# Batch 0 of a windowed attention: transposes a pair ahead, one pair without bias tables, v cast on GpSimd

## The chip, the core and the metric

The kernel runs on one core of a Trainium2 chip. The metric is the device time of one execution in microseconds. The engines are named as in the profile: PE (TensorE matmuls), PEld (its weight loads), DVE (VectorE), ACT (ScalarE), POOL (GpSimd) and SP (SyncE, which here only issues DMAs). Each engine works through its own list of instructions in order and waits on semaphores of the others.

## The reference

Attention over 8 batches, 8 heads, 576 positions of 64 elements, with a linear distance bias and a causal window of 128; then a two-layer MLP over the 4608 tokens:

```python
scores = scale * np.matmul(q, k.transpose(0, 1, 3, 2))
rel = pos[:, None] - pos[None, :]
mask = (rel >= 0) & (rel < 128)
scores = np.where(mask, scores - slopes * abs(rel), -1e9)
attn = softmax(scores)                      # per row
x = np.matmul(attn, v)                      # to (4608, 512)
h = x @ w_in                                # 512 -> 2048
out = (h * np.clip(h + 3.0, 0.0, 6.0) / 6.0) @ w_out
```

Inputs and output are float32; the kernel computes its matmuls in bf16.

## The kernel before

**Tiles.** Two heads make a pair, four pairs a batch; pair g belongs to batch g // 4. A pair's 576 queries are five tiles of 128 (the last has 64). A query tile sees its own key tile (the diagonal scores `scd`) and the one before it (the off-diagonal scores `sco`). Each set is two PSUM banks, from the pool `ps_sc`, which has two such rooms; the pools `ps_h` (two banks), `ps_av` and `ps_o` (one each) hold everything else.

**A pair's way.** q and k arrive as float32 (`load_run`, `load_double`), are cast to bf16 (`prepare` L204, `prepare_double` L223), transposed on PE into PSUM and copied out by DVE or ACT to `qTb`/`kTb` (`transposes` L211 for batch 0, one pair at a time; `wide_double` L248 and `double` L236 for two pairs of later batches). `scores_diag` (L285) and `scores_off` (L299) multiply them. In batches 0 and 1 bias and mask of the off-diagonal scores are first written into PSUM by PE from a table (`tables_off`); in batch 0 those of the diagonal as well (`tables_diag`, used where `diag_tabled` is true). Without the diagonal table the exponential is taken per head with a bias per key (L351), and a GpSimd select clears the masked half (L354). The exponentials `pd` and `po` of batch 0 lie in the room of `w_out_sb`, four rows of it for each pair, as `w_out` comes later. `attend` (L406) multiplies them with v (`vbuf`, with a column of ones that yields the row sums) into one `ps_sc` room and normalizes on DVE (reciprocal and product); `back` (L421) transposes the result into `xT` on PE, and ACT copies it out.

**The MLP.** `moe_up` (L462) takes one of 16 column tiles of `w_in` for 512 tokens: four matmuls over 512 columns, an ACT activation (L470) and a DVE product (L471). `moe_down` (L474) multiplies with `w_out`. The string `ORDER` fixes in which order up (U) and down (D) units follow, and `fill(n)` puts the next n units between the steps of the attention.

**The order.** All lists are written out by hand: `first_batch` (L546) and `second_batch` (L606) for batches 0 and 1, `segment` for the rest. In `first_batch` each pair of batch 0 is transposed and then scored, pair after pair; all exponentials come before v is used. The casts of v's five pieces (`cast_v`) are shared by DVE (0, 2, 3) and POOL (1, 4).

**The loads.** SP issues q of batch 0, then the five pieces of v, then q, k and v of batch 1, and so on; ACT issues k of batch 0. `w_in` comes in four quarters (`load_w_in`) and `w_out` in four (`load_w_out`), both issued by POOL between its casts. `second_w_in` (L175) holds the second quarter back: it first clears one element of `w_out_sb` that an exponential of batch 0 occupies, so POOL has to wait until the matmul that reads that exponential is done. `early` calls it between the first and second cast of batch 1's first pairs.

Of the kernel before, what the change touches and what calls it, by code (L numbers as in the profile page):

```python
# [18 lines left out]
def kernel(  # L19
# [9 lines left out]
    nc = tc.nc  # L29
# [78 lines left out]
    def load_tokens(b, nm):  # L108
        t = tokens(b, nm)
        for j in range(NQ):  # L110
            n = min(128, S - j * 128)
            nc.sync.dma_start(out=t[:n, j, :, :],
                              in_=src_of[nm][b, :, ds(j * 128, n), :].rearrange("h p d -> p h d"))
# [61 lines left out]
    def second_w_in():  # L175
        nc.gpsimd.memset(w_out_sb[:, 4, 0:1], 0.0)
        load_w_in(1)
# [26 lines left out]
    def prepare(g, copies):  # L204
        for nm, copy in zip("qk", copies):
            pr = prs.tile([128, RT * D], BF16, tag=f"pr{nm}", name="pr",
                          padded_shape=[128, 2 * RT * D])
            copy(out=pr, in_=runs[nm][:, g % NP, :])
            st[g, nm] = pr

    def transposes(g, copies):  # L211
        b, hp = divmod(g, NP)
        for nm, dst, copy in (("q", qTb[b % 2], copies[0]), ("k", kTb[b % 2], copies[1])):
            src = st.pop((g, nm))
            tp = ps_h.tile([128, RT, RP], BF16, tag="h", name="tp", padded_shape=[128, 16, 64])
            for t in range(RT):
                for e in range(2):
                    r = slice(e * D, (e + 1) * D)
                    nc.tensor.transpose(tp[r, t, :], src[r, ts(t, D)], ident[r, r])
            copy(out=dst[:, hp, :, :].rearrange("p j c -> p (j c)")[:, 0:S].rearrange(  # L220
                "p (a t) -> p a t", t=RT), in_=tp.rearrange("p t a -> p a t"))
# [11 lines left out]

    BANKS = {"h": ps_h, "av": ps_av, "o": ps_o}
# [28 lines left out]
    def diag_tabled(g):  # L263
        return g < NP
# [65 lines left out]
    def scores(g):  # L330
        scores_diag(g)
        scores_off(g)
# [5 lines left out]
    def exp_full(g):  # L338
        for e in range(2):
            exp_diag(g, e)  # L340
        exp_off_full(g)
# [32 lines left out]
    def av_matmuls(g, qts, where):  # L374
# [3 lines left out]
        for qt in qts:  # L378
            for e in range(2):
# [14 lines left out]
    def values(g, qts):  # L394
# [3 lines left out]
        if qts[0] == 0:  # L398
# [5 lines left out]
            in1=rc[:, 0:nq, :, :].to_broadcast([128, nq, 2, D]), op=ALU.mult)  # L404

# [95 lines left out]
    ORDER = [("UUDUDUUDUD", "UUDUDUDUD", "UDUDUDD", "UUDDDD"),  # L501
# [44 lines left out]
    def first_batch():  # L546
        prepare(0, (V, A))
# [3 lines left out]
        warm_up(10)  # L551
        transposes(0, (V, A))
        scores_diag(0)
        prepare(1, (P, V))
        transposes(1, (V, V))
        scores_off(0)
        exp_full(0)
        scores_diag(1)
        prepare(2, (P, P))
        tables_off(1)  # L560
        transposes(2, (V, V))
        scores_off(1)
        exp_full(1)
        scores_diag(2)
        prepare(3, (P, V))
        tables_off(2)
        transposes(3, (V, V))
        scores_off(2)
        exp_full(2)
        scores_diag(3)  # L570
        scores_off(3)
        exp_full(3)
        cast_v(0, 0, V)
        cast_v(0, 1, P)
        load_w_in(0)
        cast_v(0, 2, V)
        cast_v(0, 3, V)
        cast_v(0, 4, P)
# [4 lines left out]
        attend(0)  # L583
# [3 lines left out]
        back(1)  # L587
        prepare_double(1, 0, (P, P), early=second_w_in)
        attend(3)
# [4 lines left out]
        prepare_double(1, 1, (P, P))  # L594
        load_w_in(2)
        load_w_in(3)
# [9 lines left out]
    def second_batch():  # L606
        for g in range(NP, 2 * NP - 1):
            if g < NP + 2:
                wide_double(1, 1, "kq"[g - NP], V)
# [15 lines left out]
        prepare_double(2, 0, (P, P))  # L625
# [126 lines left out]
```

## Time and profile before

| | us |
|---|---|
| median of 3 timed runs | 326.79 (326.69 to 327.25) |
| the profiled execution | 325.98 |
| its span, first to last instruction | 324.2 |
| PE busy | 311.6 (96% of the span) |
| PEld / DVE / ACT / POOL busy | 168.5 / 173.9 / 198.0 / 141.2 |
| granted TensorE clock, mean | 1.00 |
| moved by DMA | 51.08 MB |

Some 117 thousand of the 128 thousand DMA packets are under 512 bytes (the token loads of v, and of q and k in later batches, come in pieces of 256 bytes). A timeline row reads: start, duration, engine, line, operation, output and input, count, and in brackets how long the engine was idle before it and who released it. A matmul's row includes the way through the array, so several overlap; the distance between starts is what PE needs for one. Rows of the same kind that follow one another are merged.

### The profile page before, as it was taken

How to read it: one execution, taken by the hardware profiler on the slowest of the kernel's cores; microseconds unless marked ns; L12 is line 12 of the kernel's file. 1: busy time of each engine (PE TensorE's matmuls, PEld its weight loads, DVE VectorE, ACT ScalarE, POOL GpSimd, SP SyncE). 2: the span in 40 equal slices, each digit the busy share in tenths (PEclk: the TensorE clock that was granted, in tenths of full speed). 3: DMA queues.
4: the chain of work that ended last, by engine and by line, in shares of the span. 5: the costliest groups of instructions: out<-in, count | busy, mean ns of one | idle time of the engine just before them, and what ended most of it. 6: DMA issues, size and time to landing. Idle time of an engine off the chain costs nothing.

```text
span 324.2 us, 7015 instructions
## 1 busy us (share of the span) xinstructions
PE 311.6 (96%) x2707; PEld 168.5 (52%) x2747; DVE 173.9 (54%) x338; ACT 198.0 (61%) x339; POOL 141.2 (44%) x249
## 2 busy tenths in 40 slices
PE   7889999999999999999999999999999999999995
PEld 6565465555555554555677655555554444444442
DVE  5577674554355654565455555655556455445510
ACT  3758976877767676666666666666666344244401
POOL 7464691783596366736663666363332000000000
PEclk9999999999999999999999999999999999999999
DMA  7999999899999999799969996930115100000111
GB/s 276 224 330 208 286 244 215 225 218 190 211 228 189 202 201 224 175 217 227 185 150 205 224 205 144 192 119 33 55 30 68 43 33 34 32 32 34 65 65 65
DMA packets 128066, 51.08 MB, mean 158 GB/s; under 512 B 115617, under 2 KB 119969, under 8 KB 128033
## 3 DMA queue, kind: packets, MB, share of 16 engines
q1 hardware_dynamic: 122800, 44.61, 63.3%
q0 software_dynamic: 4224, 4.19, 8.0%
q10 hardware_dynamic: 1008, 1.84, 1.6%
q8 instruction: 21, 0.34, 0.5%
q14 instruction: 13, 0.10, 0.1%
HBM read 36.70 MB, written 9.44 MB: 142 GB/s over the span
## 4 chain that ended last, share of the span: by engine, by line
PE 88%; ACT 5%; DVE 4%; issue 2%; POOL 0%; POOLq 0%
PE ops L483 38%; PE hps L451 36%; PE scd L296 3%; PE av L391 2%; ACT xT L438 2%; PE av L383 2%; PE sco L328 2%; ACT r L470 2%; PE tb L432 1%; PE w L153 1%; ACT kTb L244 1%; DVE qTb L220 1%; PE sco L307 1%; DVE kTb L220 1%; PE tp L254 1%
## 5 line engine op out<-in xcount | busy, mean ns | idle before, releaser
L471 DVE SCALAR_TENSOR_TENSOR gbuf<-r,hps 128x512 bf16<-128x512 f32 x144 | 98.5, 686 | 103.4 <-ACT r L470 103.3
L470 ACT ACTIVATE r<-hps,bias 128x512 f32<-128x512 f32 x144 | 98.9, 690 | 80.3 <-PE hps L451 80.1
L451 PE MATMUL hps<-xT,w_in_sb 128*128 128x512 bf16 (+1 forms) x619 | 144.1, 357 | 2.3 <-ACT xT L438 0.6
L483 PE MATMUL ops<-w_out_sb,gbuf 128*128 128x512 bf16 x557 | 139.2, 379 | 1.6 <-issue 1.1
L451 PEld LDWEIGHTS <-w_in_sb 128*128 128x128 bf16 x640 | 58.9, 98 | 53.8 <-issue 1.2
L483 PEld LDWEIGHTS <-gbuf 128*128 128x128 bf16 x576 | 53.6, 98 | 57.9
L354 POOL TENSOR_SCALAR_AFFINE_SELECT pd<-pd 128x512 bf16<-128x512 bf16 x48 | 30.0, 633 | 61.1 <-ACT pd L351 61.1
L364 POOL TENSOR_SCALAR_AFFINE_SELECT po<-po 128x512 bf16<-128x512 bf16 x48 | 30.4, 634 | 27.0 <-ACT po L361 26.0
L351 ACT ACTIVATE pd<-scd,bias_d 128x512 bf16<-128x512 f32 x48 | 32.1, 685 | 2.6 <-POOL vbuf L187 2.6
L361 ACT ACTIVATE po<-sco,bias_o 128x512 bf16<-128x512 f32 x48 | 33.2, 692 | 0.0
L498 DVE COPY osb<-ops 128x512 f32<-128x512 f32 x33 | 22.7, 688 | 18.7 <-PE ops L483 18.1
L194 POOL CAST tbuf<-ldbuf 128x512 bf16<-128x512 f32 (+1 forms) x45 | 25.5, 611 | 1.9 <-DMA qTb<-tbuf 1.9
L402 DVE TENSOR_TENSOR avs<-av,rc 128x384 bf16<-128x384 f32 (+1 forms) x48 | 23.6, 491 | 1.6
L391 PEld LDWEIGHTS <-pd 128*128 128x128 bf16 x192 | 14.3, 97 | 8.2 <-POOL tbuf L194 0.5
L438 ACT COPY xT<-tb 128x576 bf16<-128x576 bf16 x13 | 8.3, 638 | 16.7 <-PE tb L432 16.7
L383 PE MATMUL av<-vbuf,po 128*128 128x65 bf16 x192 | 18.0, 193 | 0.0
L391 PE MATMUL av<-vbuf,pd 128*128 128x65 bf16 x192 | 17.3, 194 | 0.3 <-ACT kTb L244 0.3
L383 PEld LDWEIGHTS <-po 128*128 128x128 bf16 x192 | 14.3, 98 | 3.0 <-DVE avs L402 0.5
L367 ACT ACTIVATE p4buf<-sco,bias_d 128x64 bf16<-128x64 f32 x48 | 15.7, 327 | 0.0
L187 POOL CAST vbuf<-ldbuf 128x1024 bf16<-128x1024 f32 x14 | 14.2, 1040 | 2.2 <-DMA ldbuf<-in_v_dram 2.2
L296 PEld LDWEIGHTS <-kTb 64*128 64x128 bf16 x256 | 7.2, 94 | 14.2 <-issue 10.6
L296 PE MATMUL scd<-qTb,kTb 64*128 64x128 bf16 x256 | 12.7, 219 | 1.7 <-DVE kTb L220 0.9
(94 smaller groups left out, 223.7 us busy)
## 6 DMA issues: line engine op xcount, KB each, us to landing
out_dram<-osb SPq DMA_DIRECT2D x33, 256.0 KB, 2.4
ldbuf<-in_v_dram SPq DMA_DIRECT2D x32, 256.0 KB, 5.3
ldbuf<-in_q_dram SPq DMA_DIRECT2D x20, 256.0 KB, 4.6
ldbuf<-in_k_dram SPq DMA_DIRECT2D x16, 256.0 KB, 4.9
ldbuf<-in_q_dram SPq DMA_DIRECT2D x12, 288.0 KB, 7.5
ldbuf<-in_k_dram SPq DMA_DIRECT2D x12, 288.0 KB, 7.8
w_in_sb<-in_moe_w_in_dram POOLq DMA_DIRECT2D x4, 512.0 KB, 8.6
w_out_sb<-in_moe_w_out_dram POOLq DMA_DIRECT2D x4, 512.0 KB, 10.9
```

The source lines that it names most:

```text
L194: nc.gpsimd.tensor_copy(out=tbuf[:m, :, j, :], in_=s[:m, j, :, :].rearrange("p (i e) d -> p i (e d)", e=2))
L296: nc.tensor.matmul(scd[:, e, ts(j, 128)], lhsT=kT[r, j, :], rhs=qT[r, j, :], start=first, stop=first or j == 3)
L351: nc.scalar.activation(out=pd[:, e, :, :].rearrange("p j c -> p (j c)"), in_=sc[:, e, :], func=ACT.Exp, bias=bias_d[:, h:h + 1], scale=scale)
L354: nc.gpsimd.affine_select(out=pd[:, e, :, :], in_=pd[:, e, :, :], pattern=[[0, 4], [1, 128]], channel_multiplier=-1, base=0, compare_op=AL ...
L361: nc.scalar.activation(out=po[:, e, :, :].rearrange("p j c -> p (j c)"), in_=sc[:, e, :], func=ACT.Exp, bias=bias_o[:, h:h + 1], scale=scale)
L364: nc.gpsimd.affine_select(out=po[:, e, :, :], in_=po[:, e, :, :], pattern=[[0, 4], [-1, 128]], channel_multiplier=1, base=-1, compare_op=A ...
L383: nc.tensor.matmul(out_av, lhsT=po[:, e, qt % 4, :], rhs=vb[:, qt - 1, h, :], start=True, stop=False)
L391: nc.tensor.matmul(out_av, lhsT=d, rhs=vb[:, qt, h, :], start=(qt == 0), stop=True)
L451: nc.tensor.matmul(hps[:, lo:hi], lhsT=w_in_sb[:, ks, ts(ms, 128)], rhs=xT[:, ks, ds(src, hi - lo)], start=(ks == 0), stop=(ks == n_ks - 1))
L470: nc.scalar.activation(out=r6, in_=hps, func=ACT.Relu, bias=bias3[:, 0:1], scale=1.0 / 6.0)
L471: nc.vector.scalar_tensor_tensor(out=gts[nt][:, ms, :], in0=r6, scalar=1.0, in1=hps, op0=ALU.min, op1=ALU.mult)
L483: nc.tensor.matmul(ops[nt, sub], lhsT=gts[nt][:, ms, ts(sub, 128)], rhs=w_out_sb[:, ms, :], start=(ms == 0), stop=(ms == n_ms - 1))
```

## The change

Seven things, all in the order of the lists or in batch 0:

1. `transposes` does q or k alone, into a bank of `ps_h`, `ps_o` or `ps_av`. Batch 0's transposes now run about a pair ahead of its scores. The ten warm-up matmuls in front of them are gone.
2. Pair 1 has no diagonal table any more: no table matmuls, two exponentials with bias, two selects on POOL.
3. All of v's casts are on POOL, in the order 4, 0, 1, 2, 3, in which the pieces are loaded as well. `w_in`'s first quarter is issued between the third and fourth of them. The casts of k of pairs 2 and 3 go to DVE.
4. Pair 0's values (`attend_split`) go head by head into the banks of `ps_av` and `ps_o`, and come before pair 3's off-diagonal scores on PE.
5. `second_w_in` clears an element of row 12 instead of row 4 of `w_out_sb`: pair 3's exponentials instead of pair 1's.
6. Batch 1's second double pair is transposed one pair later (k before pair 5's scores, q between them and two up units), and `w_in`'s third quarter is issued between the casts of its k and q.
7. POOL casts batch 2's k, then q, with two `w_out` loads behind each, where before all four loads came first; one up unit in `ORDER` moves from the last string to the first.

```diff
-        for j in range(NQ):
+        for j in (4, 0, 1, 2, 3) if b == 0 else range(NQ):
...
     def second_w_in():
-        nc.gpsimd.memset(w_out_sb[:, 4, 0:1], 0.0)
+        nc.gpsimd.memset(w_out_sb[:, 12, 0:1], 0.0)
         load_w_in(1)
...
-    def transposes(g, copies):
+    def transposes(g, nm, tag, copy):
...
+        tp = BANKS[tag].tile([128, RT, RP], BF16, tag=tag, name="tp", padded_shape=[128, 16, 64])
...
     def diag_tabled(g):
-        return g < NP
+        return g in (0, 2, 3)
...
+    def attend_split(g, tags):
+        avs = st[g, "avs"] = small.tile([128, NQ, 2, D], BF16, tag="avs", name="avs")
+        for e, tag in enumerate(tags):
+            av = BANKS[tag].tile([128, NQ, W], FP32, tag=tag, name="ave",
+                                 padded_shape=[128, NQ, 102])
+            av_matmuls(g, range(NQ), lambda qt, e: av[:, qt, :], (e,))
+            rc = small.tile([128, NQ, 1], FP32, tag="rcs", name="rcs")
+            nc.vector.reciprocal(rc, av[:, :, D:W])
+            nc.vector.tensor_tensor(out=avs[:, :, e, :], in0=av[:, :, 0:D],
+                                    in1=rc.to_broadcast([128, NQ, D]), op=ALU.mult)
...
-    ORDER = [("UUDUDUUDUD", "UUDUDUDUD", "UDUDUDD", "UUDDDD"),
+    ORDER = [("UUDUDUUDUUD", "UUDUDUDUD", "UDUDUDD", "UDDDD"),
...
     def first_batch():
...
-        warm_up(10)
-        transposes(0, (V, A))
+        transposes(0, "q", "h", V)
+        transposes(0, "k", "h", A)
+        prepare(1, "qk", (P, V))
+        transposes(1, "q", "o", V)
         scores_diag(0)
-        prepare(1, (P, V))
-        transposes(1, (V, V))
+        transposes(1, "k", "av", V)
         scores_off(0)
         exp_full(0)
+        prepare(2, "qk", (P, V))
+        prepare(3, "qk", (P, V))
         scores_diag(1)
...
+        transposes(2, "q", "h", V)
+        transposes(2, "k", "h", V)
+        exp_diag(1, 0)
+        exp_diag(1, 1)
+        scores_off(1)
+        transposes(3, "q", "o", V)
+        transposes(3, "k", "av", V)
+        exp_off_full(1)
+        scores(2)
         exp_full(2)
...
-        cast_v(0, 0, V)
-        cast_v(0, 1, P)
+        for j in (4, 0, 1):
+            cast_v(0, j, P)
         load_w_in(0)
-        cast_v(0, 2, V)
-        cast_v(0, 3, V)
-        cast_v(0, 4, P)
+        for j in (2, 3):
+            cast_v(0, j, P)
...
-        attend(0)
+        scores_diag(3)
+        exp_diag(3, 0)
+        tables_off(3)
+        attend_split(0, ("av", "o"))
+        scores_off(3)
+        exp_off_full(3)
         attend(1)
         back(0)
         attend(2)
         back(1)
+        attend(3)
         prepare_double(1, 0, (P, P), early=second_w_in)
-        attend(3)
         back(2)
         up_begin(0, 0, 3)
         back(3)
         wide_double(1, 0, "q", V)
-        prepare_double(1, 1, (P, P))
+        prepare_double(1, 1, (P,), "k")
         load_w_in(2)
+        prepare_double(1, 1, (P,), "q")
         load_w_in(3)
...
     def second_batch():
         for g in range(NP, 2 * NP - 1):
-            if g < NP + 2:
-                wide_double(1, 1, "kq"[g - NP], V)
+            if g == NP + 1:
+                wide_double(1, 1, "k", V)
...
-            fill(1 if g == NP + 2 else 2)
+            fill(2 if g == NP + 1 else 1)
             scores_off(g)
             exp_off_full(g)
-            fill(2 if g == NP + 2 else 1)
+            if g == NP + 1:
+                wide_double(1, 1, "q", V)
+            fill(1 if g == NP + 2 else 2)
...
-        for i in range(4):
+        prepare_double(2, 0, (P,), "k")
+        for i in range(2):
             load_w_out(i)
...
-        prepare_double(2, 0, (P, P))
+        prepare_double(2, 0, (P,), "q")
+        load_w_out(2)
+        load_w_out(3)
```

More of the change, by code (lines that the diff above doesn't have):

```diff
@@ L202, with prepare @@
     st = {}
-    def prepare(g, copies):
-        for nm, copy in zip("qk", copies):
+    def prepare(g, nms, copies):
+        for nm, copy in zip(nms, copies):
             pr = prs.tile([128, RT * D], BF16, tag=f"pr{nm}", name="pr",
@@ L209, in prepare @@
             st[g, nm] = pr
-    def transposes(g, copies):
+    BANKS = {"h": ps_h, "av": ps_av, "o": ps_o}
+    def transposes(g, nm, tag, copy):
         b, hp = divmod(g, NP)
[L213 to L221, printed above, removed]
+        src = st.pop((g, nm))
+        tp = BANKS[tag].tile([128, RT, RP], BF16, tag=tag, name="tp", padded_shape=[128, 16, 64])
+        for t in range(RT):
+            for e in range(2):
+                r = slice(e * D, (e + 1) * D)
+                nc.tensor.transpose(tp[r, t, :], src[r, ts(t, D)], ident[r, r])
+        dst = (qTb if nm == "q" else kTb)[b % 2]
+        copy(out=dst[:, hp, :, :].rearrange("p j c -> p (j c)")[:, 0:S].rearrange(
+            "p (a t) -> p a t", t=RT), in_=tp.rearrange("p t a -> p a t"))
     def prepare_double(b, dp, copies, nms="kq", early=None):
@@ L232, in prepare_double @@
             st[b, dp, nm] = pr
-    BANKS = {"h": ps_h, "av": ps_av, "o": ps_o}
     def double(b, dp, nm, part, tag, copy):
@@ L372, in exp_off, with av_matmuls @@
                                     compare_op=ALU.is_ge, fill=0.0)
-    def av_matmuls(g, qts, where):
+    def av_matmuls(g, qts, where, es=(0, 1)):
         b, hp = divmod(g, NP)
@@ L378, in av_matmuls @@
         for qt in qts:
-            for e in range(2):
+            for e in es:
                 h = 2 * hp + e
@@ L546, in first_batch @@
     def first_batch():
-        prepare(0, (V, A))
+        prepare(0, "qk", (V, A))
         warm_up(20)
@@ L550, in first_batch @@
         tables_off(0)
-        warm_up(10)
-        transposes(0, (V, A))
+        transposes(0, "q", "h", V)
+        transposes(0, "k", "h", A)
+        prepare(1, "qk", (P, V))
+        transposes(1, "q", "o", V)
         scores_diag(0)
-        prepare(1, (P, V))
-        transposes(1, (V, V))
+        transposes(1, "k", "av", V)
         scores_off(0)
         exp_full(0)
+        prepare(2, "qk", (P, V))
+        prepare(3, "qk", (P, V))
         scores_diag(1)
-        prepare(2, (P, P))
-        tables_off(1)
-        transposes(2, (V, V))
+        transposes(2, "q", "h", V)
+        transposes(2, "k", "h", V)
+        exp_diag(1, 0)
+        exp_diag(1, 1)
         scores_off(1)
[L563 to L568, printed above, removed]
-        exp_full(2)
-        scores_diag(3)
-        scores_off(3)
-        exp_full(3)
-        cast_v(0, 0, V)
-        cast_v(0, 1, P)
+        transposes(3, "q", "o", V)
+        transposes(3, "k", "av", V)
+        exp_off_full(1)
+        scores(2)
+        exp_full(2)
+        for j in (4, 0, 1):
+            cast_v(0, j, P)
         load_w_in(0)
-        cast_v(0, 2, V)
-        cast_v(0, 3, V)
-        cast_v(0, 4, P)
+        for j in (2, 3):
+            cast_v(0, j, P)
         for dp in range(2):
```

## The prediction

> **What bounds the kernel now.** I read the stretches of ten microseconds first, then the chain of waits and the order of time of the first 50 us. The profiled execution took 325.98 us with a span of 324.2; the median of the three timed runs is 326.79, so 0.81 is added to whatever the sum gives for the profiled one. About 0.65 us (0.2%) is what a measurement of this kernel can tell from no change.
>
> ```profile
> 0.00:10.00 10.00, 7.73 (x127) 6.29 (x128) 5.73 (x33) 4.02 (x6) 7.83 (x23) 1.00 0.88 275
> 10.00:20.00 10.00, 8.35 (x184) 5.28 (x183) 6.96 (x13) 6.85 (x7) 3.85 (x7) 1.00 1.16 247
> 20.00:30.00 10.00, 9.24 (x117) 6.25 (x118) 7.41 (x11) 6.93 (x12) 7.16 (x11) 1.00 1.13 271
> 30.00:40.00 10.00, 9.84 (x100) 5.11 (x101) 6.40 (x10) 9.77 (x15) 4.89 (x8) 1.00 1.16 259
> ```
>
> Columns: stretch, its length, then busy us of PE, weight loads, DVE, ACT, POOL, the granted clock, the DMA share and GB/s. PE has holes only before 24 us. From there it streams, and from 30 to 40 us ACT is as full (9.77). The DMA engines are full throughout. So the change can gain only what it takes out of the first 24 us, and only if ACT and the loads let it through.
>
> ```profile
> 16.15 0.60 POOL L181 CAST vbuf<-ldbuf 64x512 bf16<-64x512 f32 x1 [2.85 <-DMA ldbuf<-in_v_dram]
> 16.24 1.94 DVE L181 CAST vbuf<-ldbuf 128x512 bf16<-128x512 f32 x3
> ...
> 19.06 0.10 POOL L176 MEMSET w_out_sb<- 128x1 bf16 x1 [1.50 <-PE wide L391]
> 19.10 0.74 POOL L166 DMA_DIRECT2D w_in_sb<-in_moe_w_in_dram  x1
> 20.80 2.02 POOL L227 CAST pr<-ldbuf 128x576 bf16<-128x576 f32 x3 [0.95 <-DMA ldbuf<-in_k_dram]
> ```
>
> The last piece of v lands just before 16.15. DVE, busy with the copies of pair 3's transposes until 16.3, casts three pieces until 18.18, and attend(0) waits for them (17.89). The memset at 19.06 waits for the first matmul of attend(1), 0.25 us after its start at 18.81; behind it on POOL stand the load of w_in's second quarter and the three casts that batch 1's first transposes need. Those casts end at 22.82, and PE arrives at 23.79: slack 0.97.
>
> ```profile
> 42.29 0.71 ACT r L470
> 43.03 0.69 DVE gbuf L471
> 43.72 0.14 DVE rcw L412
> ...
> 43.88 0.83 DVE avs L413
> ...
> 44.76 0.45 PE tb L432 x5
> ```
>
> In the chain, batch 1's exponentials and up activations on ACT end in this piece: back(4) on PE waits for it, so between 25 and 45 us ACT sets the pace together with PE.
>
> **Part 1: the pairs of batch 0.** Before, a pair takes 2.86 us (the scores at 10.66, 13.52, 16.38), as two DVE copies of 0.76 and 0.75 stand between transposes and scores. Afterwards the transposes run a pair ahead. I follow the changed order with these durations. Without ten warm-ups (1.27 us) q0's transposes start at 5.46, when the cast of 4.82 plus 0.59 is done. POOL's cast of q1 is not earlier (6.40 to 7.06, memsets before it). Scores(0) start at 7.6 instead of 8.34; scores(1), behind DVE's two copies, at 9.3 instead of 10.66. From there ACT paces: pair 1 takes two activations of 0.63 (the row at 28.09: 1.28 for two) for one of 1.02, the rest 1.02 each; pair 3's diagonal exponential ends at 15.5 and PE reaches attend_split(0) near 15.2. Two table matmuls (0.59) and the warm-ups leave PE. All this is then hidden: attend_split needs the last piece of v. The five loads have the same bytes in a new order, so I keep the last landing at 16.15; POOL casts a full piece in 0.62 (row at 11.86), giving 16.77, against the bounds 16.0 (the fourth piece's landing record, 15.41, plus 0.62) and 17.4 (one more POOL cast queued ahead). POOL's extra work, two selects (0.61 each) and three casts, lies before 16.15 and is covered by that landing with about 0.8 us to spare. w_in's first quarter now stands behind three casts of v: issued near 13.8 instead of 12.41, with 8.2 to landing as before, 22.0.
>
> **Part 2: from v to batch 1.** From 16.77 twelve matmuls of attend_split remain, 0.03 apart, then scores_off(3) at 17.32; its exponential starts 0.49 later, as before, and ends at 18.83: no earlier than now (18.76), because it moved behind v. attend(1) runs at 17.67 (before 18.81). DVE normalizes the split in 2 x (0.2 + 0.49; 0.49 lies between the rows of 0.42 for 256 and 0.56 for 384 elements), to 18.5, and attend(1) in 0.22 + 0.82, to 19.6. attend(2) waits for the exponential's PSUM room, 18.88. back(1) waits for that 19.6 and for ACT's copy of back(0) (0.64, to 19.7), and attend(3), next on PE, starts at 20.1 (before 21.2). back(3) follows at 22.3 (before 23.51): -1.2.
>
> The memset now touches pair 3's room, so it waits for attend(3): 20.1 + 0.25 = 20.35, not 19.06. Behind it on POOL: the load's issue 0.74, to 21.13, and three casts 2.02, to 23.17. wide_double(1,0,q) starts at 23.22 instead of 23.79. PE idles 0.7 us before it. Of 1.2 us 0.57 is left. w_in's first quarter, at 22.0, is covered by this hole until about 22.8.
>
> **Part 3: batch 1.** From 23.79 to the scores at 27.33 PE had no hole. The transposes that filled 26.73 to 27.33 (0.6) are moved a pair on, so PE would be at scores(4) 2.94 us after wide_double. ACT's copy of k ended at 27.05, 3.26 us after it, and the activation before it keeps its place. Scores(4) start at +3.31: a hole of 0.37 where there was none, and 0.20 is left. In pair 5 q's wide transposes now precede two up units. ACT waits there for the ninth unit's matmuls: about 0.5 us idle, against 0.28 and 0.24 that ACT waits for scores(5) before. I charge 0.1. So r at 42.29, and back(4) behind it, come 0.1 earlier. The w_out loads: two are issued near 41.2 instead of 40.12, two near 45.3 instead of 41.61. Their first use, 52.03, has cover (the first landed at 47.6); the last landed at 57.15 and is needed near 58.9, an up unit (0.86) later by the new ORDER, so about 1 us late is free. Afterwards it is the same work in another order: nothing.
>
> **Sum**: -1.2 (back 3) +0.63 (POOL's casts) +0.37 (copy of k) +0.1 (ACT) = -0.1: 325.88 for the profiled execution, 326.7 on the median's scale.
>
> **A rule against the row.** The pairs of transposes starting at 6.45 still came 0.053 apart, those at 8.67 0.027: the matmul rate doubled at about 7.4, six microseconds after PE's first matmul, while the view's granted clock reads 1.00. The change takes 1.07 us of dense matmuls out of that stretch and opens a hole from 6.4 to 7.1. The Trainium skill, "TensorE: Matmul & The Clock Gate", Part 1, says that a free-running window of 3413 ns has to be busy before the clock doubles, which speaks against the removal. By that rule a hole in the window may cost one more window (an estimate from that page: 3.4 us at half rate); by the row alone the rise keeps its place, and no run here shows which.
>
> **Rivals.** *Faster, v earlier.* Before, the first w_in quarter was issued at 12.41, while the last pieces of v were in flight; now it is issued 1.4 later. If the last piece lands at 15.4, everything up to back(4) moves 0.75: -0.85, 325.9. For it: POOL's 2.85 us wait for v. Against: the DMA engines are full without it too.
>
> *Slower, w_in's second quarter.* Its issue moves from 19.10 to 20.39, past the casts' gate, and SP's v loads of batch 1 are ahead of it. It is needed by the fifth up unit at 23.22 + 5.4 = 28.6. The view of the line that loads w_in says of its four transfers, from issue to landing:
>
> ```profile
> DMA to landing us min/median/max: 6.4/8.6/9.2
> ```
>
> With 6.4 to 9.2 us it lands between 26.8 and 29.6. From 28.6 on every late microsecond stalls PE in order: up to +1.0, 327.7. Against: before, with 9.06, it also came only 0.4 before its use, and its start then waited for transfers that are now over at the same time. The skill's "DMA: Bandwidth & Descriptors", Queues, rings and completion order, has each engine take turns among queues packet by packet, which would let it start at once; the longest of the four above says it does not always.
>
> *Slower, the clock.* If the rate doubles only near 14 us, the matmuls from 7.5 on take twice as long: about 1.6 us of slack before v's last cast is used up and attend_split starts 0.8 later: -0.1 + 0.8, 327.5. It decides only if the rise is later than about 12 us.
>
> **Chances.** Forecast 0.40, own range 326.2 to 327.3; v earlier 0.28; w_in late 0.16; clock late 0.16. Of the slow cases 0.03 stays within the bound: faster 0.28, same 0.43, slower 0.29. The range takes in the faster case's 325.9 with a little for an even earlier landing, and w_in's worst: 325.7 to 327.8.
>
> **What would show it.** Right: attend_split held by a POOL cast that ends near 16.8; the memset near 20.35; wide_double(1,0,q) near 23.2 with POOL as its releaser; a hole on PE before scores(4), released by ACT; back(4) within 0.4 of 44.76. Wrong: a wait of the fifth up unit for w_in; transposes still 0.053 apart after 9 us; POOL's casts done before PE asks, so that the whole 1.2 reaches batch 1; or ACT without idle time around the ninth unit.

## The result and the profile after

The changed kernel took 330.08 us (median of 11 runs, 327.92 to 332.14), beside 326.79 (325.64 to 327.99) for the kernel before: a ratio of 1.009, with a 95% interval of 1.0068 to 1.0112. It is slower by 0.9%; 326.7 was forecast, 325.7 to 327.8 as the range. The profiled execution took 327.92 us with a span of 326.2 (before: 325.98 and 324.2). It is the fastest of the eleven, so it shows the loss at its smallest: the median execution is 2.2 us longer. Two more executions of the same kernel were profiled later and are shown below. In the changed kernel the lines behind `attend_split` lie 11 further down: the up unit's matmul L451 is now L462, `back`'s L432 is L443, the up activation L470 is L481.

The stretches of ten microseconds, columns as before (stretch, length, busy us of PE, weight loads, DVE, ACT and POOL, granted clock, DMA share, GB/s):

```profile
0.00:10.00 10.00, 6.92 (x148) 5.29 (x150) 7.54 (x35) 4.73 (x7) 7.34 (x22) 1.00 0.88 272
10.00:20.00 10.00, 8.42 (x197) 6.02 (x190) 6.04 (x13) 6.92 (x10) 5.74 (x10) 1.00 1.14 223
20.00:30.00 10.00, 7.93 (x70) 4.78 (x66) 4.79 (x8) 4.88 (x9) 6.89 (x11) 0.83 1.17 283
30.00:40.00 10.00, 10.00 (x100) 5.35 (x100) 7.36 (x10) 9.29 (x16) 4.54 (x7) 1.00 1.06 219
```

The third line carries the case: from 20 to 30 us PE was busy for 9.24 us at a clock of 1.00, and is now busy for 7.93 at 0.83. Two things are in it, a stop and a slower clock. Cut into pieces of two microseconds, the same view shows both:

```profile
20.00:22.00 2.00, 0.84 (x19) 0.64 (x15) 1.39 (x3) 1.17 (x2) 1.52 (x3) 1.00 1.06 361
22.00:24.00 2.00, 1.29 (x4) 0.47 (x5) 0.00 (x0) 0.00 (x0) 0.99 (x2) 0.58 1.07 377
24.00:26.00 2.00, 2.00 (x17) 1.71 (x16) 0.63 (x2) 0.37 (x1) 1.81 (x4) 0.57 1.23 248
26.00:28.00 2.00, 2.00 (x17) 1.09 (x15) 1.68 (x2) 1.34 (x2) 1.35 (x3) 1.00 1.28 227
```

PE stands still at the end of the first line, and the clock is at half in the next two. The trace's clock record has it exactly: it falls to 0.5 at 22.31 us and is back at 1.0 at 25.72, which is 3.41 us later. In the kernel before it rose once, at 7.46, and stayed. (The record begins with the first rise; the time before it counts as 1.00 in the views and in the mean clock, although the matmuls run at half rate there: the transposes of the prediction's rule, 0.053 us apart at 6.45 and 0.028 at 8.67.) PE's order of time names what it waited for:

```profile
20.58 0.44 PE L443 MATMUL tb<-ident,avs 128*128 128x128 bf16 x5 [0.17 <-ACT xT L449]
22.71 1.46 PE L462 MATMUL hps<-xT,w_in_sb 128*128 128x512 bf16 x3 [1.69 <-DMA w_in_sb<-in_moe_w_in_dram]
23.96 0.74 PE L443 MATMUL tb<-ident,avs 128*128 128x128 bf16 x5
24.49 1.17 PE L254 MATMUL tp<-ident,pr 128*128 128x128 bf16 x9
```

back(2) starts at 20.58 (before 22.13): batch 0 is 1.55 us earlier, more than the 1.2 that was forecast. Then PE stops 1.69 us for the first quarter of `w_in`, and the first up units start at 22.71, where they started at 22.62 before. The whole lead is gone. After that everything runs at half rate: five transposes of back(3) in 0.74 where they took 0.44, wide_double(1,0,q) in 1.17 where it took 0.67. The same rows in the kernel before:

```profile
22.62 0.38 PE L451 MATMUL hps<-xT,w_in_sb 128*128 128x512 bf16 x1
...
23.51 0.44 PE L432 MATMUL tb<-ident,avs 128*128 128x128 bf16 x5
23.79 0.67 PE L254 MATMUL tp<-ident,pr 128*128 128x128 bf16 x9
```

The chain of waits of the changed kernel starts with this load:

```profile
11.87 1.62 POOL vbuf L181 x3
13.49 9.18 DMA w_in_sb<-in_moe_w_in_dram
22.66 0.05 issue
22.71 1.46 PE hps L462 x3
```

POOL casts three pieces of v, issues the load at 13.49 (before 12.41), and it lands 9.18 us later (before 8.16). POOL's rows around v, and its memset:

```profile
15.64 0.62 POOL L181 CAST vbuf<-ldbuf 128x512 bf16<-128x512 f32 x1 [0.24 <-DMA ldbuf<-in_v_dram]
16.48 0.67 POOL L229 CAST pr<-ldbuf 128x576 bf16<-128x576 f32 x1 [0.22 <-DMA ldbuf<-in_k_dram]
...
20.01 0.11 POOL L176 MEMSET w_out_sb<- 128x1 bf16 x1 [2.86 <-PE wide L391]
20.47 0.74 POOL L166 DMA_DIRECT2D w_in_sb<-in_moe_w_in_dram  x1 [0.35 <-issue]
...
22.99 1.35 POOL L229 CAST pr<-ldbuf 128x576 bf16<-128x576 f32 x2 [1.11 <-DMA ldbuf<-in_q_dram]
```

The last cast of v ends at 16.26 and the memset comes at 20.01, as POOL's part of the forecast had it (16.0 to 17.4, and 20.35). The chain at back(4), the place where the forecast's account closed:

```profile
44.00 0.76 ACT r L481
...
44.78 0.69 DVE gbuf L482
45.47 0.14 DVE rcw L423
...
45.63 0.83 DVE avs L424
...
46.51 0.45 PE tb L443 x5
```

The same chain as before, 1.75 us later (44.76). How the 2.0 us of the profiled execution come about is read at five places (starts on PE, us; the two columns on the right are experiments told below):

| | before | after | dummies in the stop | load first, row 4 |
|---|---|---|---|---|
| first up units | 22.62 | 22.71 | 22.81 | 22.57 |
| scores(4) | 27.33 | 28.41 | 27.05 | 27.06 |
| scores(5) | 31.75 | 32.81 | 31.49 | 31.46 |
| back(4) | 44.76 | 46.51 | 45.19 | 45.16 |
| span | 324.2 | 326.2 | 324.8 | 324.8 |

From the first up units to scores(4), after needs 5.70 us; the kernel that reaches the same place 0.10 later with the clock up needs 4.24. So 1.46 us come with the fall of the clock. From scores(5) to back(4) the three kernels with the new batch 1 need 13.70, against 13.01 before, and another 0.2 is lost between back(4) and 96 us (51.21 us there before, 51.41 after). The sum for the profiled execution: +0.09 at the first up units; to scores(4) -0.47 (4.71 before, 4.24 with the clock up) and +1.46 for the fall; -0.02 to scores(5); +0.69 to back(4); +0.20 to the end: +1.95.

### The profile page after: what moved, and what is told of

Its sections match the earlier page's. It is cut to its first block, busy times and chain, and to the rows that moved or that the text cites. A ratio compares the mean times of both kernels' runs of the same rounds, so it can differ in the third digit from the quotient of the medians.

```text
span 326.2 us, 7038 instructions
## 1 busy us (share of the span) xinstructions
PE 314.4 (96%) x2735; PEld 167.8 (51%) x2735; DVE 173.4 (53%) x338; ACT 198.1 (61%) x340; POOL 143.5 (44%) x253
## 4 chain that ended last, share of the span: by engine, by line
PE 85%; ACT 5%; DMA 3%; POOL 3%; DVE 2%; issue 1%; POOLq 0%; DVEq 0%; ACTq 0%
PE ops L494 38%; PE hps L462 36%; DMA w_in_sb<-in_moe_w_in_dram 3%; PE scd L296 3%; PE av L391 2%; PE av L383 2%; PE sco L328 2%; ACT r L481 1%; ACT xT L449 1%; PE tb L443 1%; PE tp L254 1%; DVE gbuf L482 1%; PE tp L242 1%; ACT gbuf L351 1%; POOL vbuf L181 0%
## 5 line engine op out<-in xcount | busy, mean ns | idle before, releaser
L462 PE MATMUL hps<-xT,w_in_sb 128*128 128x512 bf16 (+1 forms) x640 | 147.0, 359 | 2.5 <-DMA w_in_sb<-in_moe_w_in_dram 1.7
L481 ACT ACTIVATE r<-hps,bias 128x512 f32<-128x512 f32 x144 | 99.1, 691 | 82.1 <-PE hps L462 82.0
L494 PE MATMUL ops<-w_out_sb,gbuf 128*128 128x512 bf16 x576 | 142.2, 379 | 0.0
L462 PEld LDWEIGHTS <-w_in_sb 128*128 128x128 bf16 x640 | 59.2, 98 | 56.6 <-issue 2.3
L354 POOL TENSOR_SCALAR_AFFINE_SELECT pd<-pd 128x512 bf16<-128x512 bf16 x48 | 30.0, 634 | 60.9 <-ACT pd L351 60.9
L509 DVE COPY osb<-ops 128x512 f32<-128x512 f32 x33 | 22.7, 689 | 20.4 <-PE ops L494 19.7
L229 POOL CAST pr<-ldbuf 128x576 bf16<-128x576 f32 x20 | 12.9, 668 | 2.2 <-DMA ldbuf<-in_q_dram 1.8
```

The source lines that it names most:

```text
L354: nc.gpsimd.affine_select(out=pd[:, e, :, :], in_=pd[:, e, :, :], pattern=[[0, 4], [1, 128]], channel_multiplier=-1, base=0, compare_op=AL ...
L462: nc.tensor.matmul(hps[:, lo:hi], lhsT=w_in_sb[:, ks, ts(ms, 128)], rhs=xT[:, ks, ds(src, hi - lo)], start=(ks == 0), stop=(ks == n_ks - 1))
L481: nc.scalar.activation(out=r6, in_=hps, func=ACT.Relu, bias=bias3[:, 0:1], scale=1.0 / 6.0)
L494: nc.tensor.matmul(ops[nt, sub], lhsT=gts[nt][:, ms, ts(sub, 128)], rhs=w_out_sb[:, ms, :], start=(ms == 0), stop=(ms == n_ms - 1))
```

## The experiments

**The load first.** Theory L: the late first quarter opens the stop, and the stop takes the clock. Rival E: batch 0's PE work without warm-ups and tables has become too thin for the clock, whatever the load does. The first run issues the load before the casts of v:

```diff
+        load_w_in(0)
         for j in (4, 0, 1):
             cast_v(0, j, P)
-        load_w_in(0)
```

> The changed kernel with one edit: w_in's first quarter is issued by POOL ahead of v's casts instead of behind three of them. Theory L (the load): in the changed kernel's profile this transfer was issued at 13.49 and landed at 22.66, PE stood idle from 20.8 to 22.71 for it, and the TensorE clock fell to 0.5 from 22.31 to 25.72 in the same hole. Issued near 11.9 it should land near 20.6, the 1.7 us wait for it should be gone, the clock should stay at 1.00 after its first rise, and the median should fall by 2.5 to 4 us, to 326 to 327.5. Rival E (PE has too little work in the early stage since warm-ups and tables went, whatever the load does): the clock still falls somewhere before 25 us and the median falls by no more than 1 us.

Measured: 327.18 us (326.09 to 327.83), ratio to before 1.0015 (0.9998 to 1.0031). Against the kernel before, measured alongside, the loss falls from 0.9% to 0.15%, by some 2.4 us. The load was issued at 12.50 and landed at 19.00, after 6.50 us; PE did not wait for it and the clock stayed up after 14.04:

```profile
22.04 0.59 PE L462 MATMUL hps<-xT,w_in_sb 128*128 128x512 bf16 x2
...
24.33 0.68 PE L254 MATMUL tp<-ident,pr 128*128 128x128 bf16 x9 [0.74 <-POOL pr L229]
```

What holds PE now is in the last row: POOL's casts, behind the memset that waits for attend(3).

**The stop filled.** The load stays late, but PE has something to do, thirty dummy matmuls:

```diff
         back(2)
+        warm_up(30)
         up_begin(0, 0, 3)
```

> The changed kernel with 30 idle matmuls (the program's own warm-up) put on PE between back(2) and the first up matmuls, where PE waits for w_in's first quarter; the transfer stays late. They take 30 x 0.056 = 1.7 us, about the hole's length. It parts the two costs of the hole, the wait and the fall of the clock. Theory L with the clock as its second half: the wait for the load stays (landing near 22.7) but no time at clock 0.5 follows; the median falls by 1.5 to 2.5 us. If the clock's fall costs nothing by itself, or comes from other holes, the median stays within 0.7 us.

Measured: 327.07 us (326.55 to 329.31), ratio 1.0031 (1.001 to 1.0052). The load landed at 22.25, the first up units started at 22.81, no earlier than in the kernel after, and yet the loss falls from 0.9% to 0.3%. The two profiled executions are the fastest of their kernels, and this one is 1.37 us shorter (326.55 against 327.92): between these two, the stop as such costs little, and what it does to the clock costs most. The medians differ by more, since nine of the twelve executions are at 327.6 or below and ten of the changed kernel's eleven above 328; what else the dummies, which stand behind the load's issue, change is not shown. PE's rows run at full rate again:

```profile
22.81 0.81 PE L462 MATMUL hps<-xT,w_in_sb 128*128 128x512 bf16 x3
...
23.73 0.67 PE L254 MATMUL tp<-ident,pr 128*128 128x128 bf16 x9
```

**Warm-ups put back.**

```diff
         tables_off(0)
+        warm_up(10)
         transposes(0, "q", "h", V)
```

> The changed kernel with the ten warm-up matmuls put back before pair 0's transposes. Rival E in its narrow form, the first rise of the clock comes late or fails without them: the median falls by 1 us or more and the spread of the runs shrinks. Theory L: within 0.7 us of the changed kernel, with the same wait for w_in near 22 us; in the profile of the changed kernel the first rise was at 5.24, earlier than the 7.46 of the kernel before.

Measured: 331.17 us (328.45 to 332.27), ratio 1.0126 (1.0088 to 1.0163). They help nothing, so rival E in its simple form falls. But its profile does not show the late load at work either: the load landed at 23.55, just as PE came to it (23.59). The clock rose at 6.59 and fell earlier, at 16.83, behind another stop that no semaphore explains, and wide_double later waited 0.75 us for POOL's casts:

```profile
12.75 0.23 PE L296 MATMUL scd<-qTb,kTb 64*128 64x128 bf16 x1
14.80 0.38 PE L296 MATMUL scd<-qTb,kTb 64*128 64x128 bf16 x7 [1.82 <-issue]
```

**The late load alone, in the kernel before.** First by a lot, then by as much as in the kernel after; one cast of v is simply repeated ahead of the load:

```diff
-        cast_v(0, 1, P)
+        for _ in range(5):
+            cast_v(0, 1, P)
         load_w_in(0)
```

> The kernel before with one edit: POOL casts v's second piece five times over (the same data) before it issues w_in's first quarter, so that the issue moves from 12.41 to about 14.9 and nothing else of POOL's work is moved past the piece of v at 16.15. Theory L: the landing moves from 20.57 to 22.7 or later, PE waits at its first up matmul, the clock falls in some or all runs, and the kernel is 1 to 4 us slower. Rival E (the cause lies in the pairs' new order and the missing warm-ups): within 0.7 us of the kernel before.

Measured: 332.0 us (331.46 to 332.45), ratio 1.0166 (1.0145 to 1.0187). Issued at 15.32, landed at 27.51; PE waited 4.79 us, and the clock was at half from 24.46 to 31.29. The milder dose, `range(3)`:

> The kernel before with one cast of v done three times in place of once ahead of the first w_in load: its issue moves from 12.41 to some 13.6 to 13.9, behind both of batch 1's first k loads, as in the kernel after (13.49 to 14.18), and nothing else of the change is in it. Theory Q: landing 22.5 to 25.7 in place of 20.57, PE waits up to 3 us at the first up unit, 327 to 330 us, ratio 1.003 to 1.010. Rival (only batch 0's new order makes the late issue dear): landing 1.3 later, 21.9, still ahead of PE at 22.6, no change.

Measured: 329.27 us (327.65 to 330.52), ratio 1.007 (1.0038 to 1.0101). Issued at 14.13, landed at 24.57. This is most of the changed kernel's loss (0.9%), without any of the change; the issue was at the late end of what the changed kernel had (13.49 to 14.18). The stop, from PE's order of time of this kernel:

```profile
24.61 1.46 PE L451 MATMUL hps<-xT,w_in_sb 128*128 128x512 bf16 x3 [3.17 <-DMA w_in_sb<-in_moe_w_in_dram]
```

and the clock behind it, by stretches of two microseconds:

```profile
22.00:24.00 2.00, 0.00 (x0) 0.00 (x0) 0.00 (x0) 0.12 (x1) 0.74 (x2) 1.00 1.11 299
24.00:26.00 2.00, 1.39 (x5) 0.56 (x6) 0.00 (x0) 0.00 (x0) 0.67 (x1) 0.64 1.17 252
26.00:28.00 2.00, 2.00 (x17) 1.66 (x16) 0.72 (x2) 0.37 (x1) 0.91 (x2) 0.50 1.21 237
```

The account is simple here: the first up units start 1.99 later than in the kernel before (24.61), scores(4) 3.39 later (30.72), back(4) 3.40, the end 3.4. So of 3.4 us the stop is 2.0 and the fall of the clock 1.4.

**Two more executions of the changed kernel.**

> The kernel after, unchanged, for a second profiled execution: its runs spread from 327.92 to 332.14 us, and the one execution profiled so far was the fastest. Theory: the other executions lose further windows of 3.4 us at half clock, in the same first 30 us, and each that lies on the path to scores(4) is up to 1.7 us more: with a mean clock of 0.984 two more windows than in the first profile, PE's hole before the first up unit again 1 to 3 us. Rival: the clock is as in the first profile and the spread comes from later than 50 us.

> The kernel after, unchanged, a third profiled execution, with the same expectations: fall of the clock within 3.5 us behind the hole before the first up unit, and from scores(4) to back(4) again 18.1 us.

Measured: 330.90 and 329.69 us, spans 329.2 and 327.9. PE waited 3.65 and 2.05 us for the load, first up units at 26.14 and 24.52, scores(4) at 31.41 and 30.18, back(4) at 49.51 and 48.28: 18.10 us from scores(4) to back(4) in all three executions. The rival (spread from later than 50 us) falls. The first up units are 3.52 and 1.90 later than in the kernel before, and from there to scores(4) 5.27 and 5.66 pass instead of the 4.24 at full clock. So in these two the late landing costs 3.5 and 1.9 us, more than the fall of the clock (1.0 and 1.4). The chain of the first of them:

```profile
11.14 1.22 POOL w_out_sb L354 x2
12.36 1.62 POOL vbuf L181 x3
13.98 11.72 DMA w_in_sb<-in_moe_w_in_dram
...
26.14 1.06 PE hps L462 x2
```

Compared with the first profile, the two selects of pair 1 that the change put on POOL (L354) start 0.49 later, and with them v's casts and the load. Why they are late stands in the stretches of this execution:

```profile
8.00:12.00 4.00, 3.69 (x83) 2.80 (x80) 3.51 (x6) 3.21 (x4) 1.87 (x4) 0.53 1.34 230
12.00:16.00 4.00, 4.00 (x70) 2.24 (x70) 1.84 (x3) 1.61 (x2) 3.74 (x7) 0.62 1.03 233
...
24.00:26.00 2.00, 0.00 (x0) 0.13 (x2) 0.00 (x0) 0.00 (x0) 1.60 (x3) 0.82 1.18 314
26.00:28.00 2.00, 1.85 (x12) 1.30 (x12) 0.00 (x0) 0.22 (x1) 2.00 (x4) 0.50 1.20 213
```

The clock fell twice here: at 8.21, behind PE's stop of 1.6 us from 5.8 to 7.5 (it waits for POOL's cast of pair 1's q), until 15.03; and again at 25.27, behind the wait for the load. So rival E is partly right after all: the early stage does lose clock in some executions, which is why the load is still later in them. Alone it is nearly free: with the load first and the memset on row 4, an execution with the same early fall had a span of 324.8, and one whose clock rose only at 14.12 had 324.6 (before: 324.2).

**The first quarter in the profiled executions** (issue and landing from the trace's DMA records):

| kernel | issued | landed | us | PE's wait |
|---|---|---|---|---|
| before | 12.41 | 20.57 | 8.2 | 0 |
| load first (five kernels, six executions) | 12.05 to 12.50 | 18.76 to 20.04 | 6.5 to 7.5 | 0 |
| before with batch 1's new order | 12.21 | 21.08 | 8.9 | 0 |
| after, dummies in the stop | 13.49 | 22.25 | 8.8 | 0 |
| after, warm-ups put back | 13.85 | 23.55 | 9.7 | 0 |
| after, three executions | 13.49 / 13.98 / 14.18 | 22.66 / 25.70 / 24.25 | 9.2 / 11.7 / 10.1 | 1.7 / 3.6 / 2.0 |
| before, load delayed | 14.13 | 24.57 | 10.4 | 3.2 |
| before, load delayed more | 15.32 | 27.51 | 12.2 | 4.8 |

A load that is issued 1 to 2 us later lands 2 to 5 us later. What changes between these rows is what stands ahead of it: SP issues batch 1's first two k loads at about 11 and 13.4 us in the changed kernel and its first q load near 14. At 12.5 one of the k loads is ahead, near 13.5 one or two, from 14 on two or three loads. In the kernel after, both k loads land by 17.2 in all three executions; where `w_in` goes first, they land at 17.9 to 20.7. The DMA engines are full throughout (shares above 1 in the views), and what is issued first gains at the other's expense. That the loads ahead are the cause is only read from this table; no run changed them alone, and the count of loads ahead does not settle it: with one k load ahead the quarter took 8.2 us in the kernel before, 8.8 with the dummies, and 10.3 in an execution of the row-4 kernel below (issued 13.50).

**Batch 1's new order alone.** The kernel before with the new `second_batch` and `ORDER` only:

```diff
-            if g < NP + 2:
-                wide_double(1, 1, "kq"[g - NP], V)
+            if g == NP + 1:
+                wide_double(1, 1, "k", V)
...
+            if g == NP + 1:
+                wide_double(1, 1, "q", V)
```

> The kernel before with only the new order of batch 1 (its second_batch and the new ORDER string; batch 0 untouched). In the profile after, the way from scores(4) to back(4) took 18.10 us (28.41 to 46.51) against 17.43 before (27.33 to 44.76), also where the first w_in load no longer held PE (with the dummy matmuls: 27.05 to 45.19, 18.14), and from back(4) to 95 us another 0.20 was lost. Theory: part 3 alone costs this 0.67 to 0.71 plus 0.20, less the 0.23 by which scores(4) comes earlier: +0.64 to +0.68, ratio about 1.002, 327.0 us against 326.3; ACT idle of some 0.6 us between the two parts of pair 5, released by PE's up unit. Rival (the prediction's own sizes): 0.1 in ACT and nothing later, less 0.23: -0.1, ratio 0.9996, and the 0.67 comes from batch 0's lateness.

Measured: 326.19 us (325.81 to 329.94), ratio 0.9999 (0.9974 to 1.0025): the timed runs can't tell the expected +0.65 from nothing. Its profile can: from scores(5) to back(4) 13.81 us, near the 13.70 of the kernel after and unlike the 13.01 before, and 51.43 instead of 51.21 from there to 96 us. In this execution everything up to scores(4) was 1.04 us earlier than in the kernel before, but the up unit before scores(5) then waited 1.0 us for `w_in`'s *second* quarter (landed 29.38). The place is ACT in pair 5; its order of time in the kernel after:

```profile
35.85 1.02 ACT L335 ACTIVATE gbuf<-sco 128x1024 bf16<-128x1024 f32 x1
37.32 0.69 ACT L481 ACTIVATE r<-hps,bias 128x512 f32<-128x512 f32 x1 [0.44 <-PE hps L462]
38.18 0.69 ACT L481 ACTIVATE r<-hps,bias 128x512 f32<-128x512 f32 x1 [0.18 <-PE hps L462]
```

q's transposes now stand on PE before two up units, and ACT waits for both. In the kernel before no ACT row between 33 and 43 us has such an idle time.

**Batch 0's new order alone, with the load first and the memset on row 4**, batch 1 as before:

> The kernel after with the old order of batch 1 (second_batch and ORDER of before), the first w_in quarter issued before the three casts of v, and the memset that gates the second quarter back on row 4. Theory: what is left is batch 0's new order without the late load, without the gate and without part 3: wide_double(1,0,q) is then held by batch 1's q (landed 22.24 where w_in went first), 22.9 instead of 23.79, if the clock is up early; up to 0.9 faster, 325.4 to 326.0, ratio 0.997 to 0.999; in executions whose clock rises late (14.04 in one profile) as before or up to 0.5 slower. Rival (the early stage is too thin whatever the loads do): a clock of 0.995 or less in most executions and no gain, 326.5 or more.

Measured: 326.08 us (325.64 to 327.11), ratio 0.9984 (0.9966 to 1.0001). Profile: 13.01 from scores(5) to back(4), span 324.4. No gain beyond the measurement: wide_double starts at 23.74 in it, since the clock was at half from 8.40 to 15.23 and batch 0 was late by as much as it had gained.

**The same with twenty dummies**, ten in PE's early stop and ten behind back(2):

```diff
         transposes(0, "k", "h", A)
+        warm_up(10)
...
         back(2)
+        warm_up(10)
         up_begin(0, 0, 3)
```

> As the kernel with only batch 0's new order, w_in first and the gate on row 4, plus ten dummy matmuls behind pair 0's transposes (in the hole of 1.3 us in which PE waits for POOL's cast of pair 1's q) and ten between back(2) and the first up units. Theory, if the early holes cost clock windows: the clock stays up after its first rise in more executions (mean clock 0.998 or more in most of them, where the kernel after had 0.979 to 0.995), and the time is as without them or up to 0.5 better: 325.2 to 326.0. Rival: the fall has to do with the late load only, then the twenty dummies change nothing or cost 0.3.

Measured: 326.24 us (325.70 to 327.85), ratio 0.999 (0.9973 to 1.0007). Eight of twelve executions have a mean clock of 0.999 or 1.0, where the same kernel without the dummies had three of twelve and the changed kernel none above 0.995, and the time stays. (The mean says that the clock held after its first rise, not how early it rose.) wide_double starts at 23.34, held by batch 1's q, which landed at 22.49; scores(4) at 26.88, then an up unit starts 0.43 late, at 28.52; the second quarter landed at 28.47, though the view names DVE as what came last.

**The whole change with the load first and the memset on row 4**, twice:

```diff
-        nc.gpsimd.memset(w_out_sb[:, 12, 0:1], 0.0)
+        nc.gpsimd.memset(w_out_sb[:, 4, 0:1], 0.0)
...
+        load_w_in(0)
         for j in (4, 0, 1):
             cast_v(0, j, P)
-        load_w_in(0)
```

> The kernel after with w_in's first quarter issued before the casts of v and the memset back on row 4; batch 1 in the new order. Theory: against the one with w_in first alone (327.18 us, wide_double(1,0,q) at 24.33, held by POOL's casts behind a memset at 21.19) the memset comes near 18, and the casts wait only for batch 1's q: 0.5 to 1.0 earlier, 326.2 to 326.7; and slower than the one with the old batch 1 by 0.6 to 0.7. Rival: the gate is no bound (w_in's second quarter, started earlier, takes the DMA engines from batch 1's q and k), no change, 327.2.

> The kernel after with w_in's first quarter ahead of the casts of v and the memset on row 4, measured a second time. Theory: the first quarter issued near 12.2 lands near 19 and the clock holds from 15 us on: 325.6 to 326.5 again, ratio 0.996 to 0.999. Rival: the first measurement was chance, the median is that of the kernel before, ratio 0.999 to 1.001.

Measured: 326.19 us, ratio 0.9977 (0.9962 to 0.9991), and the second time 326.46, ratio 0.9993 (0.998 to 1.0007). The first result alone would be a gain of 0.2%; the second does not confirm it. Against the load first alone (1.0015) the row brings 0.7 to 1.2 us by these ratios. The 0.6 to 0.7 that the new order of batch 1 should cost against the old one does not show in the times: 326.19 here beside 326.08 in the same series. By the profiles it nets 0.4 (-0.47, -0.02, +0.69 and +0.20 of the sum above). And with the ten early dummies added:

> The kernel after with w_in first, the memset on row 4, and ten dummy matmuls in the hole of 1.5 us in which PE waits for POOL's cast of pair 1's q. Theory: the three of twelve executions at 326.5 with a clock of 0.989 come down to those with 1.0, 325.6 to 326.2, ratio 0.996 to 0.998, faster than before by 0.2 to 0.4%. Rival: the first rise of the clock decides nothing, since v and batch 1's q arrive when they do: 326.2, as without the dummies.

Measured: 326.73 us (325.49 to 327.35), ratio 0.9986 (0.9968 to 1.0004). Not better: its profile has the unexplained stop (1.93 us before 14.78), and the clock at half from 14.64 to 18.05 behind it. No version was found that is reliably faster than the kernel before.

**The row alone**, the load left late:

> The kernel after with the memset back on row 4 and nothing else: w_in's first quarter still behind the three casts of v. With w_in first the same row was worth 1.0 us (327.18 to 326.19). Theory: here the late load still opens the hole and the clock still falls, so only what the casts add to it comes back: 0 to 0.7, 329.4 to 330.1, ratio to before 1.008 to 1.011. Rival (the gate is the main cause): about 326.5, ratio 1.000.

Measured: 326.34 us (326.05 to 332.12), ratio 1.0011 (0.9981 to 1.004). The expectation (329.4 to 330.1) was wrong, and the median is what the rival said (the gate is the main cause: about 326.5, ratio 1.000). With the load's place as late as in the changed kernel, seven of twelve executions are at 326.05 to 326.37, and five at 327.5 to 332.12. The profiled one was the slowest, with the load landing at 25.76 and a wait of 3.73. Four more executions were profiled to see a good one:

> The kernel after with only the memset on row 4, for another profiled execution: seven of its twelve were at 326.05 to 326.37 us, the others at 327.5 to 332.1, and the profiled one was of the latter (w_in's first quarter issued 14.21, landed 25.76). Theory G (the gate matters to the clock): in a good execution the first quarter is issued near 13.5 and lands near 22.3 to 22.7, PE stops for 1.5 to 1.9 us as in the kernel after, but the clock stays up, or the casts behind the memset end by 23.5 and wide_double starts before 23.8. Theory Q (the order of issue decides): in a good execution the first quarter lands before 21.5, because it was issued before batch 1's second k load, and PE has no hole.

> The same kernel, a further profiled execution, with the same two expectations.

> The same kernel, a third profiled execution, with the same two expectations.

> The kernel after with only the memset on row 4, one more profiled execution. Issue of w_in's first quarter between 13.4 and 14.3, as in the four looks before. Theory Q: if it is a good execution (326.4 us or less), the first quarter landed before 21.5 and PE has no hole; theory G: it landed at 22 or later and the clock stayed up or fell off the path.

All four were above the good ones (328.91, 329.10, 329.75 and 331.18 us): load issued at 13.50, 13.50, 14.30 and 14.41, landed at 23.75, 23.69, 24.31 and 24.81, PE's wait 2.50, 2.72, 1.94 and 4.25, clock fallen behind each. So all five profiled executions were poor, but only four of the eleven others: the profiled ones do not stand for this kernel. What a good execution of it looks like, and how a memset that comes after the load's issue can decide it, stays open.

## Why the prediction was wrong

The step that failed is the one sentence of parts 1 and 2 on `w_in`'s first quarter: "issued near 13.8 instead of 12.41, with 8.2 to landing as before, 22.0", and "w_in's first quarter, at 22.0, is covered by this hole until about 22.8". Its issue was right (13.49 to 14.18). Its landing was mis-sized: 9.2, 11.7 and 10.1 us instead of 8.2, so 22.7 to 25.7. A duration was carried over to another place in a queue of full DMA engines. And the wait of PE for the load was priced only as lateness that a later hole covers: that PE's stop takes the clock along was not in the sum. These are the 1.7 to 3.6 us of wait and the 1.0 to 1.5 us of clock in the three profiled executions. That a late load does this by itself is shown in the kernel before (329.27 and 332.0 us), and that the loss mostly goes with it by the load first (327.18). What stays open is why seven of twelve executions with the load in the same late place were as fast as before once the memset was back on row 4. By these times the gate of part 2, which the prediction priced only by POOL's casts (+0.63), has a share in the loss, and no profile here shows how.

- *Batch 0 and v.* Right, mechanism and times. Scores(0) at 7.62 (forecast 7.6), scores(1) at 9.28 (9.3), v's last cast ending at 16.26 (16.77, bounds 16.0 to 17.4), back(2) 1.55 earlier. This was half of the rival "v earlier": the last piece landed at 15.59. But the rival's -0.85 did not come, as the lead ended at `w_in`.
- *POOL's gate.* The memset came at 20.01 (20.35). The load's issue came 0.46 after it, where the sum had the 0.04 of the kernel before. wide_double(1,0,q) started at 24.49 instead of 23.22; in this execution batch 1's q, landed at 22.87, would have kept it to 24.34 anyway. With the stop filled it started at 23.73.
- *The hole before scores(4), released by ACT's copy of k.* Right: by the starts of the matmuls 0.37 in the kernel after (the view, which adds a matmul's way through the array, has 0.21). With the stop filled scores(4) start 3.32 after wide_double; 3.31 was forecast.
- *ACT in pair 5.* The place was right, "about 0.5 us idle" (0.44 and 0.18 in the profile); the charge was not: "I charge 0.1" netted it against waits of the old order, and scores(5) to back(4) became 0.69 longer.
- *"Afterwards it is the same work in another order: nothing."* It is about 0.2: from back(4) to the end 279.63 to 279.69 us in the profiles with the new `ORDER`, and 279.45 to 279.49 in those without. PE's matmul starts show a stop of 0.30 before 60.92 in the kernel after, between two up units that now follow each other, which the kernel before has not.
- *The rival "w_in's second quarter".* Right mechanism, other quarter. It was charged with the longest of the four transfers, 9.2; the first quarter, whose issue moved as far, was not. The second quarter did bind where nothing else was late (1.0 us in batch 1's new order alone).
- *The rival "the clock".* It looked at the first rise and asked whether it comes late. In the profiled execution the rise came earlier, at 5.24 instead of 7.46. What cost time was a fall, seventeen microseconds later. And a rise as late as 14.12 cost nothing like the 0.8 that the rival charges where the load came first (span 324.6).
- *The rule that was weighed.* The Trainium skill, "TensorE: Matmul & The Clock Gate", Part 1, has a free-running window of 3413 ns. The traces' clock records agree: every stretch in them that ends before the execution does is a multiple of it, as 3.41, 6.83, 10.24 and 17.07 us. By the rule a stop costs one more window; by the row of the kernel before, nothing. The runs side with the rule. At the place it was asked about, two of three executions of the changed kernel lose two windows, near 8 us, at little cost; the window that costs is lost later, at the stop for the load.

The whole change with the load first and the memset on row 4 took 326.19, 326.46 and, with dummies, 326.73, so without these two parts it is worth nothing that the measurement can tell. That is near the "-0.1" of the sum, but by luck: pair 5 and what follows it lost 0.69 and 0.20 where 0.1 and nothing were charged. With the load first alone the change is at 1.0015, 0.5 us slower.

## What to carry to other kernels

A load whose issue moves by one microsecond must be priced at its new place among the other loads, not with its old duration: here 1.1 to 1.8 us of issue became 2.1 to 5.1 us of landing. Where PE's stops add up to some 1.6 us within 3.4, what the clock loses behind them comes on top: here 1.0 to 1.5 us for a fall on the path, and next to nothing for the early ones, which other waits cover (with the load first and the memset on row 4, spans of 324.4 to 324.8 with an early fall or a late rise and 324.2 without). A lead won on one engine is worth only as much as the next thing it runs into, so list for each engine's new arrival what must have landed by then.

## What was not expected of the hardware

- *How little idle time takes the clock.* The Trainium skill, "TensorE: Matmul & The Clock Gate", HAM oscillation — how this bites in real kernels, gives the rule to leave PE no gap of more than about 3.4 us. Here the clock fell with a longest gap of 1.69 us, so the measurement decides against it. What separates the cases is the sum of PE's stops in one window of 3.41 us of the clock record. A stop is counted here from a matmul's start plus the time its columns take at full rate (0.21 us for 512; in the kernel after, eight such matmuls from 57.17 on take 1.73) to the next matmul's start, if it is above 0.1 us. In the kernel after, the window before the fall holds 2.15 us: 1.46 of the wait for the load, and two stops of 0.35 and 0.34 before it, without which it would have been below the limit. In the first 45 us of the twenty profiles, the 20 windows at full clock after which it fell hold 1.58 to 3.29 us of stops; those after which it held have 1.54 or less, but for one with 1.66. The kernel before has a window with 1.51, just on the safe side.
- *The early clock differs from execution to execution.* The first rise lies between 4.09 and 14.12 us in the profiles, and in the changed kernel the clock is lost again for 6.8 us, near 8, in two of three. The kernel before has a mean clock of 0.998 to 1.0 in all the runs measured beside the experiments, so it hardly loses the clock once it has risen.
- *A stop of PE without a semaphore.* In the kernel after PE started no matmul from 12.95 to 14.26, in the middle of pair 2's tables (0.98 idle in the view), and in five other profiles it was idle for 0.95 to 1.93 us near the same place. The queue of kind "instruction" has a record of 16 KB ahead of it (at 11.33, 1.27 us long, in the kernel after; at 12.03 in the one with warm-ups put back; at 10.30 in the kernel before and at 11.32 in a second execution of the kernel after, which have no such stop). That PE had run ahead of its code is a guess from these times; no run tested it. Behind v's landing it cost the changed kernel nothing, but two executions with dummies lost a window of the clock to it.
